# A window-attention and feed-forward kernel: its instruction order planned anew, with other lengths for SyncE's DMA issues

## The chip, the cores and the metric

The kernel runs on one core of a Trainium2 chip. TensorE (PE) multiplies matrices, VectorE (DVE), ScalarE (ACT) and GpSimd (POOL) work elementwise, and SyncE (SP) issues almost all DMA transfers. Each engine takes its own instructions in the order in which they were written; engines wait for each other through semaphores. The metric is the device time of the whole kernel in microseconds (us).

## The reference

Eight batches of eight heads, 512 local and 32 global positions, head dimension 64, all in float32. Global queries see every key; a local query sees the 32 global keys and the local keys at a distance of at most 32. The heads are then joined, and a feed-forward layer without gating follows.

```
s_g   = scale * q_g @ k_all.T;             out_g = softmax(s_g) @ v_all
s_ll  = where(|i - j| <= 32, scale * q_l @ k_l.T, -1e9)
s_l   = concat(scale * q_l @ k_g.T, s_ll); out_l = softmax(s_l) @ concat(v_g, v_l)
x     = concat(out_g, out_l), heads joined     # 4352 rows of 512
h     = x @ w_in                               # 512 -> 2048
y     = (h - tanh(h)) @ w_out                  # 2048 -> 512
```

## The kernel before

**Precision.** Activations and weights of the feed-forward are held as a high and a low half (`x_hi`, `x_lo`, `w_in_hi`, `w_in_lo`, `gates`, `w_out_hi`, `w_out_lo`), and each product is made as three matmuls: high with high, high with low, low with high. The weights are loaded in 32 pieces during the first batches and split as they come (`add_weights`, L413 to L439).

**Attention.** Heads are worked on in pairs, 32 in all. The first four pairs (`first_attention`) use 128-row tiles with 224 keys and TensorE transposes. From pair 4 on (`attention`), a pair goes through these steps: `add_raw` loads K and Q into `rawkq` (SP, L681, four issues each); `add_keys` and `add_queries` turn them on DVE (L692, L704); `add_band_scores` makes the scores on TensorE (L725), and `add_band` the softmax on DVE, ACT and GpSimd (L1032 to L1046) and a turn into the tile `sq` (L1052); `add_squares` moves `sq` with sixteen SP issues (L747) to the partitions at which the product wants it; `add_values` loads V into `turned`, as `load` (L621, L631) for pairs 0 to 7 and as `windows_` (L600) for pairs 8 to 31, the latter with two issues from `v_l` and two from `v_g`; `add_products` multiplies (L788 for pairs 0 to 7, L804 for the rest) and writes `x_hi` and `x_lo`. The global queries are done for two pairs at a time (`Quad`, L930 to L950).

**Feed-forward.** The attention output of one batch is a chunk of 512 rows. A chunk has 16 hidden steps (`add_hidden`, L1119: twelve matmuls of 512 columns; L1145 for the first four steps of the first batch), each followed by tanh on ACT (L1127), the subtraction on DVE (L1130), the split into halves on ACT (L359) and GpSimd (L1136), and an output step (`add_out`, L1182: twelve matmuls). While the attention of batch b runs, the feed-forward of batch b - 1 does; x is double-buffered by batch. After the last attention the rest of the feed-forward runs alone, with a last chunk of the 256 global rows. Results leave through `wraw` (L1212).

**The order.** Nothing of this is issued as it is called. Each step is added as an operation to a planner (`Order`), with the engines that may take it, a planned length on each, a penalty in us for an engine, a due time, the things that it reads and writes and, for DMAs, the length of the transfer. `Order.run` then replays the program once in the model: of all ready operations it takes the one with the earliest start on one of its engines, to which the due time is added with the small factor `kd` (3.1e-5 us for each unit), the mode change of TensorE with `mw`, and so on. The instructions are written out in the order of the planned starts, and each engine keeps that order on the chip whatever the real durations are. Up to a planned time of 72 us the planner puts filler matmuls (L1409) into gaps on TensorE.

The numbers of the planner stand in `CFG`: a name as `o_vl2` is the offset of one step of the attention (here the load of V) in a phase of batches, `a_`, `d_`, `p_` and `s_` are penalties of an engine for a kind of work, `step`, `step1`, `p0` and `bp` set the due time of a head, `hs`, `ho`, `lag` those of the feed-forward, `wd0` and `wsp` those of the weights. A DMA operation on SP has a planned issue length, for instance

```python
add(("S", 2.25), windows_, self.due(self.C["o_vl"]), w=["vh0", "vh1"],
    res=TURNED if self.j == OWN else (), xfer=5.3)
```

which says that SP is taken for 2.25 us, and that the transfer takes 5.3 us.

Of the kernel before, what the change touches and what calls it, by code (L numbers as in the profile page):

```python
# [217 lines left out]
def kernel(ctx, tc, q_l, k_l, v_l, q_g, k_g, v_g, w_in, w_out, out):  # L218
    nc = tc.nc
    B, H, S, _ = q_l.shape  # L220
# [14 lines left out]
    OWN = 8  # L235
# [90 lines left out]
    def bank(shape, j, dt=F32):  # L326
# [6 lines left out]
        elif len(shape) == 4:  # L333
# [1 line left out]
        return t  # L335


    CFG = dict(a_g=-0.6721, a_kg=1.0132, a_ph=-0.7513, a_qs=-5.8618, a_w=-0.2261, a_wn=13.7137, a_xg=47.9552, d_g=2.6561, d_kg=45.7932,
               d_ph=11.6671, d_qh=26.732, d_qs=8.4327, d_tg=43.412, d_tp=55.745, d_w=11.7403, d_wn=-2.3155, d_xg=40.1124, d_y=48.8228, gfirst=0,
               ho=8494.8073, hs=632.0575, lag=-2496.8224, last=-1262.756, newb=2, p0=1222.225, pen=19.404, penp=21.8433, s_g=16.15, s_w=22.2289,  # L340
               step=2098.1774, step1=999.3381, lag0=-7038.8598, hs0=797.5026, tol=0.0002310614, wd0=2070.4918, wsp=-254.6204, xw=8.829787e-06,
               o_ld0=4755.5639, o_tn0=1021.8746, o_tg0=5665.8088, o_s0=-6869.5142, o_sp0=-1339.9745, o_t0=-3287.8567, o_vl0=-162.2643,
               o_pv0=3278.5944, wsp1=-170.6161, ho0=7636.819, mw=0.5367028, o_h0=6666.6064, hp=-6371.5841, bp0=4983.6125, bp1=-7891.7321,
               bp2=-6141.6586, bp3=-5681.7805, p_w=19.3689, p_kg=0.1671, mv=2.825415e-05, kd=3.108638e-05, a_sq=8.5297, o_gb=3622.6795,
               o_kl2=3702.3359, o_ql2=8984.5769, o_kt2=-8897.133, o_qt2=3010.2657, o_l2=-5746.7494, o_lp2=3182.1163, o_g2=-6863.124,
               o_tg2=6085.0427, o_sq2=-6231.2758, o_vl2=-3497.1205, o_pv2=-262.1997, o_kl1=5692.9576, o_ql1=-1940.427, o_kt1=2078.4757,
               o_qt1=8088.1019, o_l1=-8999.0555, o_lp1=6205.638, o_g1=-3530.805, o_tg1=7900.5995, o_sq1=4638.1358, o_vl1=5746.0558,
               o_pv1=2233.0989, o_g0=-4890.7445, p_bd=26.7192)

    PHASE = [{k[:-1]: v for k, v in CFG.items() if k.startswith("o_") and k.endswith(x)} for x in "012"]  # L350

# [1 line left out]
    add = order.add  # L353
# [137 lines left out]
    TURNED = ["h00", "h10", "h01", "h11", "hg0", "hg1"]  # L491
# [3 lines left out]
    class Pair:  # L495
# [98 lines left out]
        def add_values(self):  # L594
            def windows_(e, _):
                n, src = 2 * NW, v_l[self.b, 2 * self.jj]
                last = self.j + 1 == B * H // 2

                def keep(dst, x):
                    self.sent.append(nc.sync.dma_start(dst, x).ins.name)  # L600

                def rows(r0, r1, n):
                    keep(win_v[r0:r1, :n], bass.AP(src.tensor, src.offset + (r0 - (G if r0 < G else 2 * G)) * D,
                                                              [[D, r1 - r0], [G * D, n], [1, D]]))

                rows(0, G, n)
                if last:
                    rows(2 * G, 3 * G, n)
                    rows(3 * G, P, n - 1)
                else:  # L610
                    rows(2 * G, P, n)
                for h in range(2):
                    g = v_g[self.b, 2 * self.jj + h]
                    keep(win_v[G:2 * G, h * NW:h * NW + NW], bass.AP(g.tensor, g.offset, [[D, G], [0, NW], [1, D]]))

            def load(e, _):
                i, n = 2 * self.j, 2 * NT

                def rows(part, t0, t1, r0, r1):
                    src = v_l[self.b, 2 * self.jj]  # L620
                    nc.sync.dma_start(first_rows[r0:r1, part, t0:t1], bass.AP(  # L621
                        src.tensor, src.offset + (P * (t0 + part) - 32 + r0) * D, [[D, r1 - r0], [P * D, t1 - t0], [1, D]]))

                first = i == 0
                rows(0, first, n, 0, P)
                if first:
                    rows(0, 0, 1, 32, P)
                rows(1, 0, n, 0, D)
                for h in range(2):
                    g = v_g[self.b, 2 * self.jj + h]  # L630
                    nc.sync.dma_start(first_v[D:D + G, 1, h], bass.AP(g.tensor, g.offset, [[D, G], [0, NT], [1, D]]))  # L631

            if self.j < OWN:
                add(("S", 2.25 if self.j else 2.8), load, self.due(self.C["o_vl"]), w=["vh0", "vh1"], xfer=2.5 if self.j else 2.8)
            else:
                add(("S", 2.25), windows_, self.due(self.C["o_vl"]), w=["vh0", "vh1"], res=TURNED if self.j == OWN else (), xfer=5.3)

        def add_local_scores(self, *halves):

# [34 lines left out]
        def add_raw(self):  # L674
            def load(a, src):
                def fn(e, _):
                    for two in range(2):
                        x = src[self.b, 2 * self.jj + two].rearrange("(b s) d -> s b d", s=32)
                        for half in range(2):
                            p0 = 64 * two + 32 * half  # L680
                            eng[e].dma_start(raws_kq[a][p0:p0 + 32].rearrange("s (b d) -> s b d", d=32),  # L681
                                             x[:, :, 32 * half:32 * half + 32])
                return fn

            for a in range(2):
                add(("S", 1.96), load(a, (k_l, q_l)[a]), self.due(self.C[("o_kl", "o_ql")[a]]), w=[("raw", "kq")[a]], xfer=1.55)

        def add_keys(self):
            kw, u = keys[self.u], self.u
# [46 lines left out]
        def add_squares(self):  # L736
            def move(c):
                def fn(e, _):
                    x = self.squares()
                    for n in range(4):  # L740
                        if self.j < OWN:
                            k = 6 if n == 1 + c % 2 else c + n - (n > 1 + c % 2)
                            dst = turned[32 * (k % 4):32 * (k % 4) + 32, k // 4, c].rearrange("p t c -> p (t c)")
                        else:
                            k = n if c % 2 == 0 else (0, 2, 1, 3)[n]
                            dst = win_t[32 * k:32 * k + 32, c]
                        x_ = eng[e].dma_start(dst,  # L747
                                         x[n * len(x) // 4][32 * c:32 * c + 32, n % (4 // len(x))].rearrange("p a t c -> p (a t c)"))
                        self.sent.append(x_.ins.name)
                return fn  # L750

            for c in range(4):
                add(("S", 2.42), move(c), self.due(self.C["o_sq"] + c), r=self.sqk, w=[("tq", c)],
                    res=["h00", "h10", "h01", "h11"], xfer=0.78)

        def add_global_turn(self):
# [623 lines left out]
    if ng >= P:  # L1380
# [19 lines left out]
        last = Chunk(lambda: [lambda cc, t=t: t[:, cc] for t in xgs()], [("xg", cc) for cc in range(NCC)], ng, "g", global_rows, chunk.due - (60 if CFG["gfirst"] else -400))  # L1400
# [45 lines left out]
```

## Time and profile before

| | |
|---|---|
| median of three runs | 927.85 us (926.07 to 930.58) |
| the profiled execution's own time | 928.07 us |
| its span, first to last instruction | 926.3 us |
| TensorE busy | 902.6 us, 97% of the span |
| VectorE, ScalarE, GpSimd busy | 434.6, 376.8, 344.3 us |
| mean granted TensorE clock | 0.993 |

Busy times come from one profiled execution. A busy TensorE is one whose matmuls overlap in their modelled ends, so the share says where it stands still, not how fast it is. The granted clock is 1.00 at 2.4 GHz and 0.50 at 1.2 GHz.

### The profile page before, as it was taken

How to read it: one execution, taken by the hardware profiler on the slowest of the kernel's cores; microseconds unless marked ns; L12 is line 12 of the kernel's file. 1: busy time of each engine (PE TensorE's matmuls, PEld its weight loads, DVE VectorE, ACT ScalarE, POOL GpSimd, SP SyncE). 2: the span in 40 equal slices, each digit the busy share in tenths (PEclk: the TensorE clock that was granted, in tenths of full speed). 3: DMA queues.
4: the chain of work that ended last, by engine and by line, in shares of the span. 5: the costliest groups of instructions: out<-in, count | busy, mean ns of one | idle time of the engine just before them, and what ended most of it. 6: DMA issues, size and time to landing. Idle time of an engine off the chain costs nothing.

```text
span 926.3 us, 22831 instructions
## 1 busy us (share of the span) xinstructions
PE 902.6 (97%) x8814; PEld 722.0 (78%) x8814; DVE 434.6 (47%) x1511; ACT 376.8 (41%) x1043; POOL 344.3 (37%) x489
## 2 busy tenths in 40 slices
PE   8999989989999999999999999999999999999998
PEld 5778777768877887777877877768877878888896
DVE  6897886653347434563346423663327521111210
ACT  6976664532336323452325323452335422322221
POOL 6676675332234223332334313342334322222322
PEclk9999999998999999999999999999999999999999
DMA  9786564655343463344334553444334330100000
GB/s 216 199 193 182 168 175 109 141 104 99 78 92 98 95 132 72 95 97 99 76 79 116 102 108 77 96 97 90 76 78 113 73 78 1 46 1 0 35 13 23
DMA packets 287341, 88.53 MB, mean 96 GB/s; under 512 B 258304, under 2 KB 280832, under 8 KB 287232
## 3 DMA queue, kind: packets, MB, share of 16 engines
q1 hardware_dynamic: 285184, 85.96, 41.2%
q8 instruction: 69, 1.13, 0.5%
q10 hardware_dynamic: 2048, 1.11, 0.4%
q14 instruction: 40, 0.33, 0.1%
HBM read 63.42 MB, written 8.91 MB: 78 GB/s over the span
## 4 chain that ended last, share of the span: by engine, by line
PE 78%; SPq 6%; DMA 5%; DVE 5%; ACT 3%; issue 2%; POOL 0%; ACTq 0%; DVEq 0%
PE bank L1182 34%; PE bank L1119 34%; SPq L747 5%; PE bank L804 4%; PE bank L725 3%; DVE sq L433 2%; PE bank L930 1%; DMA first_q<-in_moe_w_out_dram 1%; DMA wraw<-in_moe_w_out_dram 1%; SPq L600 1%; PE bank L788 1%; DMA rawkq<-in_k_l_dram 1%; ACT prob L1037 1%; DMA turned<-in_v_g_dram 1%; ACT wraw L424 1%
## 5 line engine op out<-in xcount | busy, mean ns | idle before, releaser
L1136 POOL TENSOR_TENSOR gates<-t,gates 128x512 fp32r<-128x512 f32 x136 | 176.2, 1297 | 452.8 <-PE bank L1182 388.2
L1182 PE MATMUL bank<-w_out_hi,gates 128*128 128x512 f32 x1088 | 285.9, 396 | 2.3 <-ACT gates L359 1.5
L1130 DVE TENSOR_TENSOR t<-bank,t 128x512 f32<-128x512 f32 x136 | 93.3, 687 | 353.5 <-ACT t L1127 353.1
L1182 PEld LDWEIGHTS bank<-w_out_hi,gates 128*128 128x128 f32 x1088 | 201.0, 188 | 51.5 <-issue 6.3
L1127 ACT ACTIVATE t<-bank 128x512 f32<-128x512 f32 x136 | 81.3, 598 | 218.7 <-PE bank L1119 217.1
L359 ACT CAST gates<-t 128x512 fp32r<-128x512 f32 x136 | 84.6, 622 | 205.3 <-PE bank L1182 187.6
L1182 PE MATMUL bank<-w_out_lo,gates 128*128 128x512 f32 x544 | 151.3, 392 | 0.0
L1119 PE MATMUL bank<-x_hi,w_in_hi 128*128 128x512 f32 x432 | 121.2, 396 | 0.0
L1182 PEld LDWEIGHTS bank<-w_out_lo,gates 128*128 128x128 f32 x544 | 101.7, 188 | 22.1 <-issue 0.6
L1119 PE MATMUL bank<-x_lo,w_in_hi 128*128 128x512 f32 x432 | 118.8, 391 | 0.0
L1119 PE MATMUL bank<-x_hi,w_in_lo 128*128 128x512 f32 x432 | 118.7, 390 | 0.0
L1046 POOL TENSOR_SCALAR prob<-prob,stats 128x128 f32<-128x128 f32 x224 | 82.4, 387 | 56.9 <-DVE stats L1042 46.1
L1037 ACT ACTIVATE prob<-prob,stats 128x128 f32<-128x128 f32 x224 | 87.2, 392 | 27.0 <-DVE stats L1032 27.0
L1119 PEld LDWEIGHTS bank<-x_lo,w_in_hi 128*128 128x128 f32 x432 | 81.5, 189 | 17.6 <-issue 0.2
L1119 PEld LDWEIGHTS bank<-x_hi,w_in_hi 128*128 128x128 f32 x432 | 80.1, 189 | 18.5 <-issue 0.6
L1119 PEld LDWEIGHTS bank<-x_hi,w_in_lo 128*128 128x128 f32 x432 | 81.0, 188 | 17.3
L768 DVE STREAM_TRANSPOSE turned<-pg 32x192 f32<-32x192 f32 x144 | 53.2, 369 | 13.0 <-PE bank L804 5.5
L1052 DVE STREAM_TRANSPOSE sq<-prob 128x512 f32<-128x512 f32 x50 | 33.7, 698 | 41.2 <-DMA turned<-sq 39.8
L1032 DVE CUSTOM_DVE_ANT_0 prob<-bank,band 128x128 f32<-128x128 f32 x224 | 49.7, 285 | 0.2
L804 PEld LDWEIGHTS bank<-turned 128*32 128x32 f32 x3072 | 34.3, 113 | 17.6 <-issue 13.1
L804 PE MATMUL bank<-turned 128*32 128x32 f32 (+1 forms) x3072 | 38.1, 208 | 8.6 <-DMA turned<-in_v_g_dram 3.5
L1037 ACT ACTIVATION_READ_ACCUMULATOR prob<-prob,stats 128x1 f32 x224 | 42.3, 189 | 0.0
(142 smaller groups left out, 887.9 us busy)
## 6 DMA issues: line engine op xcount, KB each, us to landing
turned<-sq SPq DMA_DIRECT2D x400, 32.0 KB, 1.8
turned<-in_v_l_dram SPq DMA_DIRECT2D x23, 512.0 KB, 5.3
turned<-in_v_l_dram SPq DMA_DIRECT2D x32, 256.0 KB, 3.1
out_dram<-wraw SPq DMA_DIRECT2D x32, 256.0 KB, 2.4
rawkq<-in_q_l_dram SPq DMA_DIRECT2D x112, 64.0 KB, 2.7
rawkq<-in_k_l_dram SPq DMA_DIRECT2D x112, 64.0 KB, 2.7
turned<-in_v_g_dram SPq DMA_DIRECT2D x48, 128.0 KB, 4.9
wraw<-in_moe_w_in_dram SPq DMA_DIRECT2D x11, 512.0 KB, 4.4
```

The source lines that it names most:

```text
L359: (nc.scalar.copy if e == "A" else eng[e].tensor_copy)(dst, src)
L747: x_ = eng[e].dma_start(dst, x[n * len(x) // 4][32 * c:32 * c + 32, n % (4 // len(x))].rearrange("p a t c -> p (a t c)"))
L768: nc.vector.transpose(win_g[32 * g:32 * g + 32, a.two], view(pg[p0:p0 + 32, 32 * j:32 * j + 1], [(96, 6), (1, G)]))
L804: m = nc.tensor.matmul(y, win_v[:, NW * a.two + w, G * d:G * d + G], x, start=n == 0, stop=n == 7, skip_group_check=True)
L1032: nc.vector.tensor_tensor_reduce(out=x[:, t], in0=self.scores[:, t], in1=bands[0 if t == 0 else 2 if t == NT - 1 else 1], scale=-0.125, sc ...
L1037: nc.scalar.activation(x[:, t], x[:, t], AF.Exp, bias=self.st[:, t:t + 1], scale=-1.0, accum_out=self.st[:, 4 + t:5 + t])
L1046: nc.gpsimd.tensor_scalar(x[:, t], x[:, t], self.st[:, 8 + t:9 + t], 1.0, op0=ALU.mult, op1=ALU.mult)
L1119: nc.tensor.matmul(self.h[s][:, j * n:(j + 1) * n], w[:, cc, f * P:(f + 1) * P], self.x()[xi](cc)[:, :n], start=part == 0 and cc == 0 and ...
L1127: nc.scalar.activation(tt_[q], self.h[s], AF.Tanh)
L1130: nc.vector.tensor_sub(tt_[q], self.h.pop(s), tt_[q])
L1136: eng[e].tensor_sub(gg[q][1], tt_[q].rearrange("p (k c) -> p k c", k=4), f32(gg[q][0]))
L1182: nc.tensor.matmul(self.acc[tt], g[:, j * nt + tt], low_out(f) if wi else w_out_hi[:, f], start=s == 0 and k == 1, stop=last and k == 3 * ...
```

## The change

The same operations with the same tiles are handed to the planner. Three planned lengths of SP's issues change: the window loads of V from 2.25 to 3.65 us, the K and Q loads from 1.96 to 2.10 us, the moves of squares from 2.42 to 2.50 us. All other numbers of `CFG` that could be set are set anew; the search that chose them replayed the plan with disturbances, in which SP's issues were longer too. The search is not part of the kernel.

```diff
-    CFG = dict(a_g=-0.6721, a_kg=1.0132, a_ph=-0.7513, a_qs=-5.8618, a_w=-0.2261, a_wn=13.7137, a_xg=47.9552, d_g=2.6561, d_kg=45.7932,
-               d_ph=11.6671, d_qh=26.732, d_qs=8.4327, d_tg=43.412, d_tp=55.745, d_w=11.7403, d_wn=-2.3155, d_xg=40.1124, d_y=48.8228, gfirst=0,
-               ho=8494.8073, hs=632.0575, lag=-2496.8224, last=-1262.756, newb=2, p0=1222.225, pen=19.404, penp=21.8433, s_g=16.15, s_w=22.2289,
-               step=2098.1774, step1=999.3381, lag0=-7038.8598, hs0=797.5026, tol=0.0002310614, wd0=2070.4918, wsp=-254.6204, xw=8.829787e-06,
...
-               o_pv0=3278.5944, wsp1=-170.6161, ho0=7636.819, mw=0.5367028, o_h0=6666.6064, hp=-6371.5841, bp0=4983.6125, bp1=-7891.7321,
-               bp2=-6141.6586, bp3=-5681.7805, p_w=19.3689, p_kg=0.1671, mv=2.825415e-05, kd=3.108638e-05, a_sq=8.5297, o_gb=3622.6795,
...
+    CFG = dict(a_g=-0.6507, a_kg=7.3662, a_ph=-8.4207, a_qs=-0.4365, a_w=-0.1731, a_wn=16.8936, a_xg=65.5986, d_g=104.4638, d_kg=29.8319,
+               d_ph=40.4703, d_qh=26.732, d_qs=1.3604, d_tg=48.1413, d_tp=10.309, d_w=32.0115, d_wn=-7.3342, d_xg=46.4798, d_y=0.0734, gfirst=0,
+               ho=1385.8278, hs=680.0498, lag=-1734.1451, last=293.5164, newb=2, p0=2157.1309, pen=-2.1431, penp=27.8427, s_g=47.3491, s_w=45.8454,
+               step=1403.3207, step1=1380.2051, lag0=-6876.7019, hs0=1078.0705, tol=8.889322e-06, wd0=7155.0302, wsp=-113.4019, xw=0.00205136,
...
+               o_pv0=7039.7846, wsp1=-388.4399, ho0=6937.7422, mw=0.7012931, o_h0=4164.8063, hp=-2484.6799, bp0=7270.1145, bp1=-7658.3358,
+               bp2=-7100.5615, bp3=-4009.4348, p_w=2.3314, p_kg=0.5612, mv=0.0002403397, kd=3.023447e-05, a_sq=8.5297, o_gb=3906.0276,
...
-                add(("S", 2.25), windows_, self.due(self.C["o_vl"]), w=["vh0", "vh1"], res=TURNED if self.j == OWN else (), xfer=5.3)
+                add(("S", 3.65), windows_, self.due(self.C["o_vl"]), w=["vh0", "vh1"], res=TURNED if self.j == OWN else (), xfer=5.3)
...
-                add(("S", 1.96), load(a, (k_l, q_l)[a]), self.due(self.C[("o_kl", "o_ql")[a]]), w=[("raw", "kq")[a]], xfer=1.55)
+                add(("S", 2.1), load(a, (k_l, q_l)[a]), self.due(self.C[("o_kl", "o_ql")[a]]), w=[("raw", "kq")[a]], xfer=1.55)
...
-                add(("S", 2.42), move(c), self.due(self.C["o_sq"] + c), r=self.sqk, w=[("tq", c)],
+                add(("S", 2.5), move(c), self.due(self.C["o_sq"] + c), r=self.sqk, w=[("tq", c)],
```

## Rows read from the trace of the kernel before

**Rows 1.** The page, busy time of TensorE: us, share of the span, instructions.
```profile
PE 902.6 (97%) x8814; PEld 722.0 (78%) x8814; DVE 434.6 (47%) x1511; ACT 376.8 (41%) x1043; POOL 344.3 (37%) x489
```

**Rows 2.** Busy time by stage: start:end, us, each engine, clock, DMA share, GB/s.
```profile
0.00:72.00 72.00, 65.14 (x558) 49.44 (x559) 58.55 (x242) 57.86 (x174) 46.98 (x81) 0.98 0.85 199
72.00:150.00 78.00, 75.40 (x505) 59.97 (x504) 62.73 (x183) 45.98 (x112) 51.15 (x57) 0.98 0.67 179
150.00:215.00 65.00, 60.06 (x752) 46.26 (x752) 39.57 (x162) 28.29 (x98) 23.52 (x44) 0.95 0.47 102
215.00:757.00 542.00, 536.89 (x6070) 426.96 (x6069) 249.03 (x889) 202.68 (x592) 180.93 (x274) 1.00 0.43 92
757.00:926.00 169.00, 165.07 (x936) 139.40 (x934) 24.76 (x37) 42.02 (x70) 41.77 (x34) 1.00 0.08 22
```

**Rows 3.** The same view of three stretches at the lower granted clock.
```profile
35.87:39.29 3.42, 3.33 (x16) 2.92 (x15) 3.15 (x14) 2.87 (x6) 2.66 (x7) 0.50 0.84 173
121.20:124.62 3.42, 3.42 (x26) 2.88 (x23) 2.20 (x5) 2.33 (x5) 2.60 (x4) 0.50 1.02 236
206.54:213.37 6.83, 5.41 (x135) 4.69 (x136) 3.44 (x12) 2.29 (x10) 1.34 (x5) 0.50 0.50 80
```

**Rows 4.** TensorE's waits: for whom, us in total, times, longest.
```profile
PE bank L804 <- DMA turned<-in_v_g_dram: 3.5, 1, 3.5
PE bank L804 <- issue: 2.6, 2, 2.1
PE bank L788 <- DMA turned<-in_v_l_dram: 2.6, 1, 2.6
PE bank L804 <- DMA rawkq<-in_k_l_dram: 1.6, 2, 1.0
...
PE bank L804 <- DMA out_dram<-wraw: 0.8, 1, 0.8
```

**Rows 5.** Timeline of SP's queue around 200 us: start, us, issue.
```profile
194.78 5.81 SPq L747 DMA_DIRECT2D turned<-sq  x8
200.63 1.30 SPq L600 DMA_DIRECT2D turned<-in_v_l_dram  x2
201.97 2.58 SPq L600 DMA_DIRECT2D turned<-in_v_g_dram  x2
```

**Rows 6.** Timeline of TensorE at 120 us and around 208 us.
```profile
120.20 3.73 PE L788 MATMUL bank<-turned 128*64 128x160 f32 x32 [2.58 <-DMA turned<-in_v_l_dram]
...
202.31 2.11 PE L1182 MATMUL bank<-w_out_hi,gates 128*128 128x512 f32 x8
207.96 2.58 PE L804 MATMUL bank<-turned 128*32 128x64 f32 x128 [3.54 <-DMA turned<-in_v_g_dram]
```

**Rows 7.** Timeline around 325 us, a group of window loads and the product.
```profile
322.51 1.28 SPq L600 DMA_DIRECT2D turned<-in_v_l_dram  x2
...
323.83 2.12 SPq L600 DMA_DIRECT2D turned<-in_v_g_dram  x2
...
329.52 1.53 PE L804 MATMUL bank<-turned 128*32 128x64 f32 x128 [0.57 <-DMA rawkq<-in_k_l_dram]
```

**Rows 8.** SP: issues of squares, ns min/median/max; the wait of window loads.
```profile
L747 SPq DMA_DIRECT2D turned<-sq x400: 507/589/1888, 150.5 to 754.7; - x134
...
SPq L600 <- PE bank L804: 41.6, 6, 11.6
```

**Rows 9.** The page, DMA issues: count, KB each, median us to landing.
```profile
turned<-in_v_g_dram SPq DMA_DIRECT2D x48, 128.0 KB, 4.9
```

**Rows 10.** Groups on ScalarE: casts of gates and copies of results, us, mean ns.
```profile
L359 ACT CAST gates<-t 128x512 fp32r<-128x512 f32 x136 | 84.6, 622 | 205.3 <-PE bank L1182 187.6 <-DVE t L1130 15.6 <-DVE sq L1052 2.1
...
L359 ACT COPY wraw<-bank 128x512 f32<-128x512 f32 x34 | 19.9, 584 | 24.3 <-PE bank L1182 18.0 <-DMA out_dram<-wraw 5.6
```

**Rows 11.** The chain that ended last, after attention work: start, us, steps.
```profile
233.63 2.97 PE bank L1182 x12
236.59 2.74 PE bank L1119 x12
```

More of the change, by code (lines that the diff above doesn't have):

```diff
@@ L335, in bank @@
         return t
-    CFG = dict(a_g=-0.6721, a_kg=1.0132, a_ph=-0.7513, a_qs=-5.8618, a_w=-0.2261, a_wn=13.7137, a_xg=47.9552, d_g=2.6561, d_kg=45.7932,
-               d_ph=11.6671, d_qh=26.732, d_qs=8.4327, d_tg=43.412, d_tp=55.745, d_w=11.7403, d_wn=-2.3155, d_xg=40.1124, d_y=48.8228, gfirst=0,
-               ho=8494.8073, hs=632.0575, lag=-2496.8224, last=-1262.756, newb=2, p0=1222.225, pen=19.404, penp=21.8433, s_g=16.15, s_w=22.2289,
-               step=2098.1774, step1=999.3381, lag0=-7038.8598, hs0=797.5026, tol=0.0002310614, wd0=2070.4918, wsp=-254.6204, xw=8.829787e-06,
-               o_ld0=4755.5639, o_tn0=1021.8746, o_tg0=5665.8088, o_s0=-6869.5142, o_sp0=-1339.9745, o_t0=-3287.8567, o_vl0=-162.2643,
-               o_pv0=3278.5944, wsp1=-170.6161, ho0=7636.819, mw=0.5367028, o_h0=6666.6064, hp=-6371.5841, bp0=4983.6125, bp1=-7891.7321,
-               bp2=-6141.6586, bp3=-5681.7805, p_w=19.3689, p_kg=0.1671, mv=2.825415e-05, kd=3.108638e-05, a_sq=8.5297, o_gb=3622.6795,
[L345 to L348, printed above, removed]
@@ new lines @@
+    CFG = dict(a_g=-0.6507, a_kg=7.3662, a_ph=-8.4207, a_qs=-0.4365, a_w=-0.1731, a_wn=16.8936, a_xg=65.5986, d_g=104.4638, d_kg=29.8319,
+               d_ph=40.4703, d_qh=26.732, d_qs=1.3604, d_tg=48.1413, d_tp=10.309, d_w=32.0115, d_wn=-7.3342, d_xg=46.4798, d_y=0.0734, gfirst=0,
+               ho=1385.8278, hs=680.0498, lag=-1734.1451, last=293.5164, newb=2, p0=2157.1309, pen=-2.1431, penp=27.8427, s_g=47.3491, s_w=45.8454,
+               step=1403.3207, step1=1380.2051, lag0=-6876.7019, hs0=1078.0705, tol=8.889322e-06, wd0=7155.0302, wsp=-113.4019, xw=0.00205136,
+               o_ld0=7544.0828, o_tn0=-315.3719, o_tg0=2046.4822, o_s0=-3763.0672, o_sp0=-1339.9745, o_t0=-2535.4029, o_vl0=1700.5112,
+               o_pv0=7039.7846, wsp1=-388.4399, ho0=6937.7422, mw=0.7012931, o_h0=4164.8063, hp=-2484.6799, bp0=7270.1145, bp1=-7658.3358,
+               bp2=-7100.5615, bp3=-4009.4348, p_w=2.3314, p_kg=0.5612, mv=0.0002403397, kd=3.023447e-05, a_sq=8.5297, o_gb=3906.0276,
+               o_kl2=2277.7415, o_ql2=3382.2241, o_kt2=-4437.9217, o_qt2=5009.1231, o_l2=-2944.6847, o_lp2=6395.7726, o_g2=-6231.3059,
+               o_tg2=7354.6514, o_sq2=1320.4858, o_vl2=978.2486, o_pv2=1297.1393, o_kl1=-1142.5719, o_ql1=3850.6568, o_kt1=5436.5477,
+               o_qt1=-1422.8474, o_l1=-9000, o_lp1=5581.7675, o_g1=-2567.6346, o_tg1=1497.1942, o_sq1=9000, o_vl1=-5952.7958, o_pv1=2779.6983,
+               o_g0=-3261.865, p_bd=30.115)
```

## The prediction

> **What bounds the kernel now.** I read the page first, then the stages, the waits, and last single stretches. On the page TensorE is busy for 902.6 us [rows 1] of a span of 926.3 us, so an order of the same operations can win back only what TensorE stands still, plus what it runs at half clock. The view by stages says where that is [rows 2]: from 757 us on the feed-forward alone runs, and from 215 to 757 us TensorE is busy 536.89 of 542 us. The first 215 us hold 72.00 - 65.14 = 6.9, 78.00 - 75.40 = 2.6 and 65.00 - 60.06 = 4.9 us of idle time, 14.4 us together, though they are under a quarter of the span.
>
> The clock: in three stretches the granted clock is 0.50, that is 1.2 instead of 2.4 GHz [rows 3]. TensorE is busy for 3.33, 3.42 and 5.41 us in them, and half of that, 1.7 + 1.7 + 2.7 = 6.1 us, is what the lower level costs. Two of them go with idle stretches of TensorE, which stood still for 2.58 us before 120.20 and for 3.54 us before 207.96 us [rows 6].
>
> Who keeps TensorE waiting is the fourth view [rows 4]. The largest are two loads of V: `turned<-in_v_g_dram` 3.5 us ahead of L804, `turned<-in_v_l_dram` 2.6 us ahead of L788. L804 also loses 1.6 us in two waits put down to `rawkq` loads and 0.8 us in one put down to an output store, and 2.6 us in two pieces called issue, in which it waits for no semaphore that the profile shows. A wait on a DMA here is a wait on SP, which issues almost every load one after the other.
>
> The stretch around the largest wait shows how [rows 5]. SP issues without a hole: the eight moves of squares end at 194.78 + 5.81 = 200.59 us, the window loads start at 200.63 us and take until 201.97 + 2.58 = 204.55 us. TensorE has its last ready matmuls from 202.31 to 204.42 us, and the next instruction of its queue is the product, which starts at 207.96 us [rows 6]. One such load takes 4.9 us from issue to landing [rows 9], and the first of the two v_g loads is issued at 201.97 us: the landing is no slower than usual, the issue came too late. Hidden matmuls stand behind the product in TensorE's queue, which is in order, and run only after it.
>
> **The change, part by part.** No operation is added or removed, and no tile changes; what differs is the planner's input, so each instruction may move, with its DMAs.
>
> *The lengths of SP's issues.* The window loads are planned at 3.65 instead of 2.25 us. In the trace one group takes from 322.51 to 323.83 + 2.12 = 325.95, 3.44 us [rows 7], and the one at 200.63 us takes 3.92 us [rows 5], so the old figure is short by 1.2 to 1.7 us and the new one is near the rows. Moves of squares go from 2.42 to 2.50 us: four at the median of 589 ns are 2.36 us without the gaps between them [rows 8]. Raw loads go from 1.96 to 2.10 us. There are 24 groups of window loads, 112 of squares and 56 of raw loads, so the plan's SP becomes 24 x 1.40 + 112 x 0.08 + 56 x 0.14 = 33.6 + 9.0 + 7.8 = 50 us longer. The chip's SP takes that time today already, so this costs nothing by itself; it moves the place at which the planner believes a load to have landed, by up to 1.4 us for each window load ahead in the queue. What it can be worth is the waits of L804 on DMAs, all of them behind window loads, since L804 is the product from pair 8 on: 3.5 + 1.6 + 0.8 = 5.9 us [rows 4], plus the 2.7 us of half clock that follow the first [rows 3], 8.6 us in all. Below, the gain is zero: the longest single issue of a square is 1888 against a median of 589 ns [rows 8], and where such outliers made the lateness, a mean length does not cure it. I take the large wait as gone with its half clock (3.5 + 2.7 = 6.2), because the plan now holds the overrun of the window load before it and the product has hidden matmuls to change places with, and half of the 2.4 us of small ones (1.2): 7.4 us.
>
> The Trainium skill, in DMA: Bandwidth & Descriptors, section Issuing engines are not separate DMA queues, speaks against this part: it holds the sequencer's time to initiate a DMA to be usually small relative to the DMA itself. By that rule correct issue lengths would move nothing that matters, and the sum would be 928 instead of 922. The trace does not agree here: a group of four issues takes 3.44 us [rows 7] where one landing takes 4.9 us [rows 9].
>
> *What is queued on SP.* A window load waits for the products that read the last windows (41.6 us in six waits of up to 11.6 us [rows 8]), and everything behind it in SP's queue, raw loads and squares, waits too. If the new order issues a window load earlier in the queue, the raw loads behind it stand still until that product is done; their cover is the feed-forward, of which each pair has four hidden and four output steps, 4 x (2.97 + 2.74) = 23 us [rows 11]. Cost taken: nothing; if the cover fails, one raw load of 1.0 us more a batch, as one of the two waits of 1.6 us together showed.
>
> *The offsets of the first 160 us.* The due times of weights, first products and hidden steps of the first chunk all move, by 0.1 to 0.3 us of start time each, since a due time enters with a factor of 3e-5 (`wd0`: 5085 x 3e-5 = 0.15 us). The waits there are the 2.6 us at 120.20 with 1.7 us of half clock, and 1.7 us of half clock at 35.87 us [rows 3, 4], 6.0 us that a new order could lose or double; nothing in the trace says which. I take zero, and keep both ends.
>
> *The engines' penalties.* DVE's penalty for the casts of gates goes to 104 us: all 136 are on ScalarE already [rows 10]. DVE's for the output copies goes from 48.8 to 0.07, so some of the 34 copies of 584 ns leave ScalarE [rows 10]; they are covered by matmuls except for the last, where the difference is of the order of 0.1 us. GpSimd may take high halves of weights: covered by the weights' lead as long as the first hidden steps find them. Nothing is taken for these; without cover, one late weight costs what a late load costs, up to 2.6 us [rows 4].
>
> *Changes of operation on TensorE.* The penalty for a change of mode rises from 0.54 to 0.70 us. A step of twelve matmuls behind attention work takes 2.97 us, one behind its like 2.74 us [rows 11], so a change costs 0.23 us. The pairs make 28 + 24 + 16 + 8 = 76 groups of L725, L804, L930 and L788, and each must still be entered and left; joining five of them would be worth 1 us. I take zero, with 1 us as the end.
>
> *New waits of the new order.* Where products and loads change places, some new order will be late elsewhere. I price this by one wait as the longer of the two put down to raw loads, 1.0 us [rows 4].
>
> Sum: 928.07 (the profiled execution's own time) - 7.4 + 1.0 = 921.7, so 922. The own time lies 0.2 us above the median of the three runs, which is left out. Best end: 8.6 + 6.0 + 1.0 saved, 912. Worst end: two new waits as the largest one, each with its half clock, 2 x 6.2 = 12.4 on top of nothing gained, 940.
>
> **The rivals.** *A, nothing to be measured.* The lateness comes from single long issues and from pieces without any semaphore (2.6 us), which no mean length in a plan removes, and the new offsets only move the waits. For it: SP's outliers [rows 8], and that the steady stage has only 5.1 us of idle time to give [rows 2]. Against it: the largest wait stands in a stretch of plain, unbroken issues [rows 5]. Time: 928.
>
> *B, slower.* A product is queued ahead of ready hidden matmuls, early on, before its load has landed. The place is the stretch from 72 to 215 us, where V, squares, raw loads and weights share SP; the price is a wait as that at 207.96 with its half clock, 3.5 + 2.7 = 6.2 us. It decides where a load lands as late as at 120.20 or 207.96 us, 2.6 to 3.5 us after TensorE has run out: both of these waits went with the lower clock [rows 3, 6]. For it: two such waits exist in an order that was made by the same planner. Against it: the longer lengths push products back, not forward. Time: 928 + 6 = 934.
>
> *C, the change does not do what it says.* The new lengths are right, but the greedy planner takes the earliest start at every step, and a later landing in the plan merely puts a product after matmuls that were to come next anyway. Then L804's small waits stay, and the time is within 2 us of 928; it goes with A.
>
> **How the numbers follow.** Forecast 0.48, A with C 0.32, B 0.20. The forecast's own range is 918 to 925, half of the gain lost or the early stage helping by its half. The change that a measurement of this kernel can tell is 0.5%, 4.6 us: below 923.2 or above 932.5. Of the forecast's 0.48, 0.43 lies below 923.2; B lies above 932.5 in 0.18 of its 0.20; the rest is the same. The range takes in B's price and a gain that reaches the start: 913 to 934.
>
> **What would show it.** Right: no wait of L804 on a `turned` load above 1 us, no stretch at half clock after 150 us, window loads that start before TensorE's last ready step, and TensorE idle in 150 to 215 us down from 4.9 to about 1.5 us. The matmul counts, and the 169 us of the last stage, stay as they are. Wrong for A: the waits at other places but of the same sum. Wrong for B: another wait above 2.5 us before 215 us, with the clock at 0.50 behind it. The prediction also fails if the first 72 us, which it holds equal, move by more than 3 us.

## The result, and the profile after

The changed kernel takes 919.15 us (median of four runs, 918.3 to 920.23), against 927.34 us for the kernel before in as many runs beside it: a ratio of 0.991, 95% interval 0.988 to 0.994. The forecast was 922 us.

The view by stages of the changed kernel, with the columns of [rows 2] (the stretch, its length, the busy time of TensorE, its weight loads, VectorE, ScalarE and GpSimd, then clock, DMA share and GB/s):

```profile
0.00:72.00 72.00, 64.01 (x546) 47.13 (x547) 57.84 (x243) 56.33 (x174) 45.70 (x81) 0.98 0.84 200
72.00:150.00 78.00, 73.35 (x498) 58.28 (x497) 66.86 (x168) 46.39 (x110) 50.34 (x56) 0.98 0.64 171
150.00:215.00 65.00, 65.00 (x606) 50.93 (x607) 37.92 (x144) 26.65 (x84) 23.74 (x36) 1.00 0.47 104
215.00:757.00 542.00, 542.00 (x6260) 431.26 (x6260) 254.94 (x917) 203.50 (x604) 184.98 (x288) 1.00 0.43 92
37.72:41.13 3.41, 3.41 (x16) 2.65 (x18) 2.77 (x6) 3.21 (x6) 1.35 (x3) 0.50 0.83 172
129.88:133.29 3.41, 3.41 (x52) 2.54 (x36) 3.28 (x19) 2.44 (x10) 2.04 (x2) 0.50 0.92 220
```

Beside [rows 2] the reader sees two things. From 150 to 757 us TensorE has no idle time left, where it had 4.9 + 5.1 = 10.0 us. In the first 150 us it has more than before, 7.99 + 4.65 = 12.6 instead of 9.5 us. The last two rows answer to [rows 3]: two stretches at half clock are left, worth 3.4 us instead of 6.1, and the one around 208 us is gone. The sum is 10.0 - 3.2 + 2.7 = 9.5 us won, and the two spans differ by 926.3 - 918.5 = 7.8 us: 1.3 us are lost again in the work itself (three more fillers are part of it) and 0.4 us in idle time behind 757 us.

TensorE's waits in the changed kernel, against [rows 4] (for whom, us in total, times, longest):

```profile
PE bank L1182 <- ACT gates L359: 2.8, 2, 1.8
PE bank L725 <- DVE xg L830: 2.0, 1, 2.0
PE bank L582 <- POOL pg L950: 1.7, 1, 1.7
PE bank L788 <- DVE kw L692: 1.6, 1, 1.6
```

L804 is no longer in the list, neither with loads nor with the pieces called issue. What is left up to 757 us stands in the first 130 us.

### The profile page after: what moved, and what is told of

The parts are those of the page before. It is cut to its first block, busy times and chain, and to the rows that moved or that the text cites. A ratio compares the mean times of both kernels' runs of the same rounds, so it can differ in the third digit from the quotient of the medians.

```text
span 918.5 us, 22826 instructions
## 1 busy us (share of the span) xinstructions
PE 901.2 (98%) x8817; PEld 720.1 (78%) x8817; DVE 443.0 (48%) x1519; ACT 371.8 (40%) x1035; POOL 342.8 (37%) x489
## 4 chain that ended last, share of the span: by engine, by line
PE 88%; DVE 5%; DMA 3%; ACT 2%; issue 1%; POOL 1%; SPq 0%; ACTq 0%; DVEq 0%; POOLq 0%
PE bank L1119 38%; PE bank L1182 38%; PE bank L804 4%; PE bank L725 3%; PE bank L930 2%; DVE sq L433 1%; DMA wraw<-in_moe_w_in_dram 1%; PE bank L788 1%; DMA rawkq<-in_k_l_dram 1%; PE bank L651 1%; DVE first_q L428 1%; PE bank L1076 1%; DVE turned L763 1%; DMA raw<-in_q_l_dram 0%; ACT prob L1037 0%
## 5 line engine op out<-in xcount | busy, mean ns | idle before, releaser
L1182 PE MATMUL bank<-w_out_hi,gates 128*128 128x512 f32 x1088 | 295.9, 392 | 2.8 <-ACT gates L359 2.8
L1119 PE MATMUL bank<-x_hi,w_in_hi 128*128 128x512 f32 x432 | 125.3, 406 | 0.0
L1119 PEld LDWEIGHTS bank<-x_hi,w_in_lo 128*128 128x128 f32 x432 | 81.1, 188 | 17.7
L1119 PEld LDWEIGHTS bank<-x_hi,w_in_hi 128*128 128x128 f32 x432 | 77.8, 189 | 21.3 <-issue 5.0
L804 PEld LDWEIGHTS bank<-turned 128*32 128x32 f32 x3072 | 33.1, 111 | 8.5 <-issue 8.5
L804 PE MATMUL bank<-turned 128*32 128x32 f32 (+1 forms) x3072 | 36.9, 206 | 0.0
```

The costliest lines, as they stand in the source:

```text
L804: m = nc.tensor.matmul(y, win_v[:, NW * a.two + w, G * d:G * d + G], x, start=n == 0, stop=n == 7, skip_group_check=True)
L1119: nc.tensor.matmul(self.h[s][:, j * n:(j + 1) * n], w[:, cc, f * P:(f + 1) * P], self.x()[xi](cc)[:, :n], start=part == 0 and cc == 0 and ...
L1182: nc.tensor.matmul(self.acc[tt], g[:, j * nt + tt], low_out(f) if wi else w_out_hi[:, f], start=s == 0 and k == 1, stop=last and k == 3 * ...
```

## The experiments

Every kernel runs beside the kernel before on one chip, and the ratio is that of the two. The work itself takes nearly the same in all: span minus idle time of TensorE minus half of its busy time at half clock is 896 to 899 us in the 14 profiles. Behind 757 us all have 4.2 to 4.6 us of idle time. A span can therefore be read as these two plus three things that differ: idle time up to 215 us, idle time from 215 to 757 us (the steady stage), and half clock, which is half of TensorE's busy time at the lower clock. The table gives them from each kernel's one profiled execution, while the ratio is that of all its runs; the distances are the feed-forward matmuls of 512 columns between one product L804 and the next, for the four pairs of a batch in the middle of the run, counted in the order of TensorE's instructions.

| kernel | ratio (interval) | idle to 215 us | idle 215 to 757 us | half clock | distances |
|---|---|---|---|---|---|
| before | 1 | 14.4 | 5.1 | 6.1 | 64, 88, 104, 128 |
| after | 0.991 (0.988 to 0.994) | 12.6 | 0.0 | 3.4 | 96, 96, 84, 108 |
| e1 | 1.003 (1.000 to 1.006) | 15.1 | 4.5 | 9.1 | 64, 88, 104, 128 |
| e2 | 0.995 (0.992 to 0.998) | 17.0 | 0.0 | 6.4 | 96, 96, 84, 108 |
| e3 | 1.004 (1.002 to 1.007) | 15.9 | 6.3 | 3.4 | 64, 88, 104, 128 |
| e4 | 0.990 (0.987 to 0.993) | 13.8 | 0.0 | 1.7 | 96, 96, 84, 108 |
| e5 | 0.993 (0.990 to 0.996) | 12.9 | 0.9 | 3.4 | 64, 88, 104, 128 |
| e6 | 1.013 (1.009 to 1.018) | 22.5 | 4.9 | 7.4 | 56, 72, 128, 128 |
| e7 | 0.994 (0.992 to 0.996) | 15.3 | 0.0 | 3.3 | 96, 96, 84, 108 |
| e8 | 1.004 (1.000 to 1.007) | 15.2 | 7.9 | 8.1 | 64, 88, 104, 128 |
| e9 | 1.000 (0.998 to 1.003) | 15.9 | 0.0 | 9.5 | 96, 96, 84, 108 |
| e10 | 1.016 (1.013 to 1.019) | 16.6 | 17.8 | 5.1 | 64, 68, 160, 92 |
| e11 | 0.991 (0.988 to 0.994) | 13.6 | 0.0 | 3.4 | 96, 96, 84, 108 |
| e12 | 0.995 (0.993 to 0.997) | 17.7 | 0.0 | 1.7 | 96, 96, 84, 108 |

**The lengths alone (e1), and all but the lengths (e2).** The theory of the prediction is that the true lengths in the plan put the products behind their loads. Its rival is that the offsets do it.

```diff
# e1: the kernel before          # e2: the changed kernel, the reverse
-add(("S", 2.25), windows_, ...
+add(("S", 3.65), windows_, ...
-add(("S", 1.96), load(a, (k_l, q_l)[a]), ...
+add(("S", 2.1), load(a, (k_l, q_l)[a]), ...
-add(("S", 2.42), move(c), ...
+add(("S", 2.5), move(c), ...
```

> The kernel before with the three new issue lengths alone (window loads 3.65, raw loads 2.10, squares 2.50 us), all offsets old. Lengths theory (the prediction's): the products are planned behind the true landing, so L804's waits on turned loads fall from 3.5 us to under 1 us, no half clock stands around 208 us, and the time is 919 to 923 us. Offsets theory: the lengths do little by themselves and the gain came with the new offsets; L804 and L788 keep waits of 4 us or more in sum and the time is 925 to 930 us.

> The changed kernel with the three old issue lengths (2.25, 1.96, 2.42 us), all offsets new. Lengths theory: products are again planned ahead of their loads, waits of L804 of 4 us or more come back after 150 us, and the time is 924 us or more. Offsets theory: the waits after 150 us stay below 1.5 us in sum and the time stays at 918 to 921 us.

With the new lengths alone the kernel is 0.3% slower, which the interval barely tells from no change, and 4.5 of the 5.1 us of idle time from 215 us on remain. With the old lengths the changed kernel keeps the steady stage without any wait, against the lengths theory, but loses about half of its gain before 215 us, against the offsets theory, which had expected 918 to 921 us. The waits of e2 (columns as above):

```profile
PE bank L1182 <- ACT gates L359: 4.7, 3, 2.1
PE bank L788 <- DMA turned<-sq: 3.1, 2, 1.9
```

Both theories miss one half. The orders of the instructions, made by replaying the plan with one length changed at a time, say more. With the window loads at 2.25 instead of 3.65 us, all else as in the changed kernel, every engine has the same instructions in the same order; with 3.65 instead of 2.25 us in the kernel before, too. The edit that the prediction held for the heart of the change changes no instruction. The raw loads' length moves nothing in the kernel before, and in the changed one a few instructions of VectorE and ScalarE. Only the squares' 0.08 us reorder TensorE, and with the new offsets by a step: 2.42, 2.43, 2.45 and 2.47 us give one order of TensorE's instructions, and 2.48, 2.50 and 2.58 us another. In the code, `Order.run` splits a planned length into `int(d / 0.55 + 0.5)` issues: 4 up to 2.47, 5 from 2.48 on. That step is not the only thing that reorders: with the old offsets 2.43 us already gives another order than 2.42 (e3), and with the new ones 2.70 another than 2.50 (e12), at the same number of issues. All of these reorder TensorE early on only: before, e1, e3, e5 and e8 have one order of TensorE from the second product L804 on (at 208 us in the kernel before), and after, e2, e4, e7 and e12 have another from the first product on. Why the window loads' length moves nothing stands in the code: a transfer lands at `max(at["Q"], s + d + 0.6) + o.land`, with `at["Q"]` at least `s + 1.06 + 5.3` for a window load. So 6.36 us behind the start stands against 2.85 us with the old length and 4.25 with the new one, and in the replayed plans none of the 24 window loads starts or lands later by it. That the loads behind them on SP hardly move either (in the changed kernel's plan none lands otherwise) I put down to the same 5.3 us in the modelled transfer queue, which is argued only.

**A hundredth of a microsecond (e3).**

```diff
-add(("S", 2.42), move(c), ...
+add(("S", 2.43), move(c), ...
```

> The kernel before with one planned length moved by a hundredth: squares at 2.43 instead of 2.42 us. It is a control for what a mere reshuffle of the order does. Lengths theory: a hundredth of a microsecond carries no knowledge, so the time is within 2 us of the kernel before, 925 to 930 us, with about 10 us of waits on loads. A rival of both, that the time of an order is a draw: it differs from the kernel before by 3 us or more, and its waits stand in other places.

0.4% slower, some 4 us, so the rival of both has its case: a length that carries no knowledge moves the time as much as the three new ones do in e1. The waits stand elsewhere (2.5 us at 234.46 us, where the kernel before has none), and in the steady stage TensorE is idle for 6.3 us. The profile does not hold the loss, though: its three terms add up to 25.6 us, as in the kernel before, and its execution took 929.18 us where the ten took 927.91 to 935.66. The granted clock of the ten is 0.991 in the mean, against 0.994 in the 29 runs beside them; by that share of 900 us of busy TensorE, an estimate, some 3 of the 4 us are half clock.

**SP relieved (e5), in the order of the kernel before.** The values of the global keys are left out of every pair after pair 8.

```diff
-                for h in range(2):
+                for h in range(2 if self.j == OWN else 0):
                     g = v_g[self.b, 2 * self.jj + h]
```

> The kernel before in its own order, without the two v_g issues of each window group after pair 8; the global values of the later pairs are left out, and SP is relieved of about 2 us a pair. If SP's lateness is what L804 waited for, its waits on turned, rawkq and out_dram loads (5.9 us) fall below 1 us, the half clock at 206 us is gone, and the time falls by 6 to 9 us to 918 to 921 us. If the waits come from something else (single long issues, the matmuls' own issue), less than 3 us is gained.

The kernel is 0.7% faster, and this in an order of compute that is the same instruction for instruction. The 3.5 us wait at 208 us shrinks to 1.0, the half clock after it is gone, and the steady stage has 0.9 us of idle time. Not all of it went: L804 still waits 1.8 us at 186.56 us. The pieces called issue shrink from 2.6 to 0.7 us, so most of that was probably SP's lateness too, though the profile put no semaphore to it; e8, with more loads on SP, has 1.6 us of it, which does not fit. The edit shortens the transfers as well as the issues, so it shows the lateness of loads, and not which of the two made it.

```profile
PE bank L804 <- DMA rawkq<-in_k_l_dram: 1.8, 1, 1.8
PE bank L804 <- DVE stats L1042: 1.0, 1, 1.0
PE bank L804 <- issue: 0.7, 1, 0.7
```

**The place in SP's queue (e6, e7).** In the kernel before, SP issues most window loads behind the pair's squares, right ahead of the product [rows 5, 7]; in the changed one, ahead of them. SP's timeline of the changed kernel around the pair of 346 us, and the product on TensorE:

```profile
323.26 1.20 SPq L600 DMA_DIRECT2D turned<-in_v_l_dram  x2
324.50 2.14 SPq L600 DMA_DIRECT2D turned<-in_v_g_dram  x2
326.74 10.42 SPq L747 DMA_DIRECT2D turned<-sq  x16
```
```profile
346.46 1.54 PE L804 MATMUL bank<-turned 128*32 128x64 f32 x128
```

The last issue ends at 326.74 + 10.42 = 337.16 us, 9.3 us ahead of the product; in [rows 7] the window loads end at 325.95 us, 3.6 us ahead of it, less than the 4.9 us that one takes to land [rows 9]. That looked like the cause, and two offsets set it.

```diff
# e6: the kernel before
-o_vl2=-3497.1205, ... o_vl1=5746.0558
+o_vl2=-9000, ... o_vl1=-9000
# e7: the changed kernel
-o_vl2=978.2486, ... o_vl1=-5952.7958
+o_vl2=9000, ... o_vl1=9000
```

> The kernel before with two offsets alone changed, o_vl1 and o_vl2 to -9000, so that SP issues each group of window loads ahead of the pair's squares and no longer behind them; all lengths old. Queue-place theory: the product's window loads land more than 10 us before it everywhere from 215 us on, TensorE's idle time from 215 to 757 us falls from 5.1 us to under 1 us, and the time is 918 to 923 us. Rival, that the many offsets together made the gain: under 2 us is gained, 925 us or more, and waits of L804 of over 3 us remain.

> The changed kernel with two offsets alone changed, o_vl1 and o_vl2 to 9000, so that SP issues the window loads behind the pair's squares, as in the kernel before; all lengths new (3.65, 2.10, 2.50 us). Queue-place theory: the slack between landing and product falls to under 2 us in many pairs; as the plan knows the lengths, waits of some 3 to 8 us come back between 150 and 757 us, and the time is 922 to 928 us. Lengths theory: with the true lengths in the plan the products are placed behind the landing, no waits come back and the time stays at 918 to 920 us.

The theory falls in both directions. In e6 the window loads go first as planned, and the product now waits for the squares, as the first two rows show; the idle time from 215 us on stays at 4.9 us, and a wait of 10.2 us of L788 on squares before 215 us makes the kernel 1.3% slower. This is not a clean test of the place, as the two offsets also shorten the short distances, from 64 and 88 to 56 and 72 matmuls. e7 is: its distances are those of the changed kernel, its window loads go last and end at 338.55 + 2.40 = 340.95 us, 8.5 us ahead of the product, and the steady stage still has no idle time. What it loses against the changed kernel, 2.7 us of idle time, lies before 215 us; the intervals of the two ratios overlap.

```profile
324.75 10.83 SPq L747 DMA_DIRECT2D turned<-sq  x16
```
```profile
337.19 1.03 PE L804 MATMUL bank<-turned 128*32 128x64 f32 x79 [1.29 <-DMA turned<-sq]
```

The wait of e6 before 215 us, then SP and the product in e7:

```profile
PE bank L788 <- DMA turned<-sq: 10.6, 2, 10.2
```
```profile
326.01 11.17 SPq L747 DMA_DIRECT2D turned<-sq  x16
337.23 1.28 SPq L600 DMA_DIRECT2D turned<-in_v_l_dram  x2
338.55 2.40 SPq L600 DMA_DIRECT2D turned<-in_v_g_dram  x2
```
```profile
349.47 0.74 PE L804 MATMUL bank<-turned 128*32 128x64 f32 x52
```

**More issue time than planned (e4, e8).** Each group of window loads issues two small loads more, into columns that nothing reads; each kernel keeps its own order.

```diff
                     keep(win_v[G:2 * G, h * NW:h * NW + NW], bass.AP(...))
+                    nc.sync.dma_start(region[:G, 2 * NW * (D + G) + 12 * G + h * D:...],
+                                      bass.AP(g.tensor, g.offset, [[D, G], [1, D]]))
```

> The changed kernel in its own order with two more small SP issues (4 and 4 KB read, 8 KB each) in each group of window loads, which the plan does not know: SP takes about 1 us longer a pair. Queue-place theory: the loads land 12 us or more ahead of the product, the squares 3 us or more, so the time moves by less than 1 us.

> The kernel before in its own order with the same two extra SP issues in each group of window loads. Queue-place theory: about half of the products wait for a window load that lands 0.2 to 1 us ahead of them, so each 0.5 to 1 us that SP is later is paid in full there: 4 to 12 us slower. If SP's issue time does not reach TensorE: less than 2 us.

The changed kernel does not notice: 0.990 against 0.991, no wait of L804. The kernel before gets 0.4% slower by the ratio, 3.3 us where 4 to 12 were expected. Its waits of L804 on raw loads rise from 1.6 to 9.4 us, as the profile now puts down to them those that it put down to window loads; all waits of L804 together rise from 8.5 to 12.1 us, and the idle time from 215 us on from 5.1 to 7.9 us:

```profile
PE bank L804 <- DMA rawkq<-in_k_l_dram: 9.4, 4, 4.5
```

**The pace (e9, e10, e11).** What e7 and the changed kernel have in common is the distance of the products. TensorE's products L804 of one batch in the kernel before, and below them in the changed one:

```profile
287.01 1.54 PE L804 MATMUL bank<-turned 128*32 128x64 f32 x128
307.25 1.54 PE L804 MATMUL bank<-turned 128*32 128x64 f32 x128
...
356.10 1.54 PE L804 MATMUL bank<-turned 128*32 128x64 f32 x128
```
```profile
295.43 1.54 PE L804 MATMUL bank<-turned 128*32 128x64 f32 x128
321.66 1.54 PE L804 MATMUL bank<-turned 128*32 128x64 f32 x128
...
370.02 1.54 PE L804 MATMUL bank<-turned 128*32 128x64 f32 x128
```

With 329.52 of [rows 7] the kernel before has 20.2, 22.3 and 26.6 us between them, the changed one, with 346.46, has 26.2, 24.8 and 23.6 us. Over the whole run the mean distance is nearly the same, (779.5 - 185.4) / 23 = 25.8 us in the kernel before and (776.7 - 193.0) / 23 = 25.4 us in the changed one. SP needs 10.8 us for the squares of a pair, 3.4 for its window loads and 4.3 for the raw loads of the next, 18.5 us in all, plus the loads of the globals once a batch. Where the distance is 20 us, SP has no hole between two products, and the product comes as soon as SP is done. Here is SP ahead of the two short distances of the kernel before:

```profile
299.27 1.29 SPq L600 DMA_DIRECT2D turned<-in_v_l_dram  x2
300.61 3.34 SPq L600 DMA_DIRECT2D turned<-in_v_g_dram  x2
304.04 2.19 SPq L681 DMA_DIRECT2D rawkq<-in_k_l_dram  x4
306.27 2.08 SPq L681 DMA_DIRECT2D rawkq<-in_q_l_dram  x4
308.45 3.14 SPq L858 DMA_DIRECT2D qgt<-in_q_g_dram  x4
311.70 10.76 SPq L747 DMA_DIRECT2D turned<-sq  x16
```

Each row starts where the one before ends. Five offsets, the due times of heads and of feed-forward steps, set the pace; the order of other work moves with them. e9 puts the five new ones alone into the kernel before, e10 puts the old ones back into the changed kernel, e11 is e9 with the three new lengths.

```diff
# e9: the kernel before; e10 is the reverse in the changed kernel
-ho=8494.8073, hs=632.0575, lag=-2496.8224, step=2098.1774, step1=999.3381
+ho=1385.8278, hs=680.0498, lag=-1734.1451, step=1403.3207, step1=1380.2051
```

> The kernel before with five of the new offsets alone (ho, hs, lag, step, step1: the due times of heads and of feed-forward steps); all lengths and all other offsets old. In the order of the instructions they change how many feed-forward matmuls stand between one product L804 and the next: 96, 96, 84, 108 for the four pairs of a batch, as in the changed kernel, where the kernel before has 88, 104, 128, 64. Pace theory: with even distances SP has time for each pair, every load lands some microseconds before its product, TensorE's idle time from 215 to 757 us falls from 5.1 us to under 0.5 us, and the time is 918 to 924 us, depending on the first 215 us. If the pace is not it: idle time of 3 us or more stays there, 925 us or more.

> The changed kernel with the five old offsets (ho, hs, lag, step, step1), new lengths and all other offsets new. The distances between products are then 68, 160, 92, 64 matmuls. Pace theory: the pairs with 64 and 68 matmuls ahead of them find their loads just landed or late, 3 us or more of idle time come back from 215 to 757 us, and the time is 923 to 932 us. Lengths theory: the plan knows SP's true lengths, so no waits come back whatever the pace, and the time is 918 to 921 us.

> The kernel before with the same five offsets and the three new lengths. If the lengths matter once the pace is even, it is in the first 215 us, where the squares of the first pairs share SP with weights and V: 2 us or more faster than the same kernel with the old lengths. If they do not, the two differ by less than 2 us, or the one with new lengths is slower; both have under 0.5 us of idle time from 215 to 757 us.

The steady stage does what the pace theory says: e9 and e11 have no idle time there, e10 has 17.8 us and is the slowest kernel of all, beyond what was expected. In e10 the waits also stand where the theory wants them: from 215 to 757 us all nine products L804 with 64 or 68 matmuls ahead of them wait, for 0.7 to 5.3 us each (one of them, by the profile, for VectorE), and of the eleven with 80 or more one does, for 0.3 us. The stage from 215 to 757 us in e9 and in e10, and most of e10's waits:

```profile
215.00:757.00 542.00, 542.00 (x6150) 431.06 (x6150) 255.95 (x911) 204.59 (x608) 184.11 (x283) 1.00 0.43 91
```
```profile
215.00:757.00 542.00, 524.24 (x5943) 415.99 (x5942) 247.22 (x891) 199.09 (x588) 177.66 (x272) 1.00 0.43 91
```
```profile
PE bank L804 <- DMA turned<-sq: 13.1, 8, 2.6
```

SP in e9 still issues the window loads behind the squares, but it has holes, here from 516.25 + 1.85 = 518.10 to 525.01 us:

```profile
516.25 1.85 SPq L858 DMA_DIRECT2D qgt<-in_q_g_dram  x4
525.01 11.13 SPq L747 DMA_DIRECT2D turned<-sq  x16
```

But e9 as a whole is no faster than the kernel before. It loses before 215 us what it gains behind, by the table 1.5 us of idle time and 3.4 us of half clock. There stand a wait of L725 on VectorE of 3.4 us at 121.65 us, 2.4 us of L788 on squares, 1.7 us of the first product L804 on a raw load at 192.90 us, and 9.5 us by half clock. e11, with the same pace and the new lengths, is 0.9% faster than the kernel before: it has 3.4 us of half clock, 1.3 us of L725 and no wait of L804, but 2.6 us of L788 on squares. The waits of e9:

```profile
PE bank L725 <- DVE t L1130: 3.4, 1, 3.4
PE bank L788 <- DMA turned<-sq: 2.4, 2, 1.9
PE bank L804 <- DMA rawkq<-in_k_l_dram: 1.7, 1, 1.7
```

**A longer plan still (e12).**

```diff
# the changed kernel
-add(("S", 2.5), move(c), ...
+add(("S", 2.7), move(c), ...
```

> The changed kernel with the planned length of the squares raised once more, from 2.50 to 2.70 us, longer than the 2.48 us that the trace shows; all else as in the changed kernel. The pace of the products is the same. If a longer planned length is a margin that keeps the first 215 us safe: no wait stands from 150 to 215 us, TensorE is idle there for under 1 us, and the time is 917 to 921 us. If the order of the first 215 us is a draw that each new length makes afresh: waits of 2 to 5 us stand between 150 and 215 us, as in the kernel with the old lengths, and the time is 922 to 928 us. In both, the stage from 215 to 757 us has no idle time.

The ratio is 0.995, and there are 2.8 us of idle time between 150 and 215 us where the changed kernel has none. A longer planned length is no margin by itself; the order of the first 215 us came out worse. The stage from there on is without idle time again.

```profile
150.00:215.00 65.00, 62.16 (x596) 48.17 (x591) 38.19 (x142) 25.20 (x77) 22.14 (x31) 1.00 0.44 99
215.00:757.00 542.00, 542.00 (x6154) 431.44 (x6153) 256.24 (x922) 205.76 (x612) 187.00 (x291) 1.00 0.43 92
```

No kernel is clearly faster than the changed one: e4's ratio of 0.990 lies within its interval, and e4 only adds work.

## Why the prediction was right, and where its reason was wrong

**The sum.** The forecast was 6.4 us, 7.4 won and 1.0 lost. Won from L804's waits on DMAs and the half clock behind the largest were all 5.9 + 2.7 = 8.6 us, the prediction's upper end for this term; also won were the 2.6 us of L804 called issue, which it had counted as out of reach. Lost were 3.2 us of idle time before 150 us, priced at 1.0 us. So 3.8 us more were won than forecast and 2.2 us more lost. The forecast's time is off by little because these two cancel in part, and its largest term, the wait at 208 us, was not won by the cause it names: this wait is gone with the old lengths too (e2). That the time came out so near is luck in this sense, and no sign that the reason was right.

**The step that failed** is "The lengths of SP's issues", in its cause. The prediction reasoned that each window load, planned 1.4 us too short, makes the planner believe in too early a landing. That the loads were late is right, and e5 shows it. That the planned length made them late is wrong: of the three lengths, that of the window loads moves no instruction in either kernel and not even its own planned landing, that of the raw loads moves next to none, and the squares' reorders TensorE, with the offsets of either kernel, only ahead of the steady stage. What removed the waits from 215 us on is the pace, set by five offsets, which the prediction did not cost at all. All seven kernels with distances of 84 to 108 matmuls have 0.0 us of idle time there (after, e2, e4, e7, e9, e11, e12; five of them with one order of TensorE), the six with distances down to 56 or 64 and a full SP have 4.5 to 17.8 us (before, e1, e3, e6, e8, e10), and e5, with the short distances but a relieved SP, has 0.9. e9 and e10 change the five offsets alone, in both directions. More loads on SP add 2.8 us at the uneven pace (e8) and nothing at the even one (e4), fewer take 4.2 us away (e5), so it is SP's load against the distance that counts here. Whether the issues of these loads or their transfers do it the three edits cannot tell, as they change both; SP's rows without a hole ahead of the short distances speak for the issues.

**The Trainium skill's rule**, in DMA: Bandwidth & Descriptors, section Issuing engines are not separate DMA queues, was that a DMA's initiation is usually small relative to the DMA. For the planned length of the window loads its outcome came true, no change, for another reason than the rule's. For a single DMA the trace bears it out: one issue of a v_g load in [rows 7] takes 2.12 / 2 = 1.06 us, against 4.9 us to landing; the prediction had set four issues against one landing. What the rule leaves out is the sum in one queue: 18.5 us of issues a pair are a limit wherever a pair has 20 us.

**Rival A** held that the waits come from single long issues that no plan removes. Wrong for the steady stage: all are gone, though single issues are as long as before (a square up to 1822 ns, against 1888; a v_g load 904 ns in the median and up to 3072, against 929 and 3189). **Rival B**, a product ahead of its load early on, did not come in the changed kernel, but it is what e6 shows, with 10.2 us of L788 on squares and half of 11.3 us at half clock. Its price of 6.2 us was too low there. **Rival C**, that the new lengths change nothing that counts, was right for the window loads, though not for its reason, that a later landing leaves the order as it is: in the plan they land no later. For TensorE it was right for the raw loads too, but not for the squares.

**The first 215 us.** Of the gain, 1.8 us of idle time and 2.7 us of half clock lie here. No single cause is shown. The pace may account for the wait at 208 us, at the second product L804: ahead of that product stand 64 matmuls in before and e8, and 52 in e6, with waits of 3.5, 4.5 and 1.9 us (and of 1.0 us in e5, with 64), and 84 to 96 in the seven even kernels, with none. But e10, with 64, and e1 and e3, with 72, have none either. Over the 14 kernels idle time there runs from 12.6 to 22.5 us and half clock from 1.7 to 9.5 us; a hundredth of a microsecond in one length (e3) or 0.2 us in another (e12) moves the time by 4 us. The new lengths help in two comparisons (after against e2, e11 against e9) and hurt in one (e1 against before), the first and the last by little more than the runs can tell; in the first two comparisons TensorE's orders differ through the squares' step alone. Whether the searched offsets fit the new lengths here, or the changed kernel's order came out well by chance, is left open.

**What was to be seen.** No wait of L804 on a `turned` load, no half clock after 150 us, and idle time from 150 to 215 us at 0.0 us, where 1.5 was expected. Window loads start 23 us ahead of the product in the pair shown. The first 72 us moved by 1.1 us of idle time, within the 3 us allowed. Of the output copies nine moved to VectorE, at 688 ns each instead of 587, with no wait of TensorE on them.

## What to carry to other kernels

Where one queue feeds a stage, compare the time that it needs for one unit of work with the shortest distance between two consumers, not with the mean: here SP needed 18.5 us a pair, the mean distance was 26 us, and the pairs at 20 to 23 us paid for it. When a planner's input changes, compare the orders that it makes before explaining a gain by the input: an edit that moves no instruction has no effect, however right it is. And judge one retuned order against neighbours that differ by nothing that should matter; here these alone moved the time by 0.4%.

## What the runs showed of the hardware

Idle time called issue, with no semaphore in the profile, need not be the engine's own: the 2.6 us of L804 went to 0.7 us when SP was relieved, to 1.6 us when it had more to do, and to nothing at an even pace. One program's time also spreads: the kernel before took 922.31 to 933.77 us in 29 runs beside e1, e2, e3 and e5, so that the changes of 0.3 to 0.4% above rest on their intervals and not on single runs. Its half clock spreads too: the granted clock of these 29 runs is 0.988 to 0.999, so the half clock of one profile is that of one execution. In e6 the wait of 10.2 us went with 20.5 us at the lower clock, of which TensorE was busy for 11.3 us.

```profile
163.96:184.44 20.48, 11.31 (x106) 8.68 (x107) 8.18 (x36) 3.56 (x12) 2.25 (x6) 0.50 0.54 136
```
